# A weight load cut in two, later numerators and paired first tiles in a linear-attention and MoE kernel

## The chip, the cores and the metric

The kernel runs on one core of a Trainium2 chip. The metric is the device time of one execution in microseconds (us), taken as the median of several executions.

TensorE is called PE below, VectorE DVE, ScalarE ACT, and GpSimd POOL. L387 is line 387 of the kernel. The changed kernel has a few lines more, so later lines move (L444 is L447 there, L608 is L618), but the lines that matter here, L164 to L396, are the same in both.

## The reference

```python
phi(x) = where(x > 0, x, exp(x) - 1) + 1
q_p, k_p = phi(q), phi(k)                       # q, k, v: 8 batches, 8 heads, 576, 64
kv  = einsum('bhsd,bhse->bhde', k_p, v);  z = sum(k_p, axis=2)
num = einsum('bhsd,bhde->bhse', q_p, kv)
den = einsum('bhsd,bhd->bhs', q_p, z)[..., None] + 1e-6
x   = (num / den), as 4608 tokens x 512
h   = x @ w_in                                  # 512 x 2048
out = (h - tanh(h)) @ w_out                     # 2048 x 512
```

## The kernel before

The 4608 tokens go through the two dense layers in 9 chunks of 512. A chunk has 16 slots of layer 1 (a tile of 128 hidden features each, four matmuls over the pieces p of xT) and 16 slots of layer 2 (four matmuls each). The attention of later batches is hung onto these slots as lists of functions, `s1` and `s2`, so that PE always has dense matmuls between the small attention steps.

All inputs are loaded by POOL's queue, in the order in which they are issued (order of the first 25 us, cut):

```python
load_k(1); load_wo(0); load_wo(1); load_q(1)
...
load_v(1)
load_wo(2)          # w_out rows 1024..1535: the third quarter, features fi = 8..11
load_wo(3)
```

Layer 2 of chunk 0 goes quarter by quarter over four output tiles; later chunks go tile by tile. Before the third quarter stands the attention of batch 1:

```python
s2[7].append(lambda: (a_qT_pe(1, 0, side), a_kv(1, side), a_qT_pe(1, 1, side)))
...
for s in range(16):
    (g, i) = divmod(s, 4) if c == 0 else (s % 4, s // 4)
    ...
    l2mm(gT, os_[i], i, 4 * g, 4 * g + 4)     # four matmuls, L387
    if g == 3:
        evac(c, i, os_[i])                    # ACT copy, L396, then the store
    for f in s2[s]:
        f()
```

`a_qT_pe` transposes q (L164) and `a_kv` multiplies k and v (L177). In chunk 1 the numerators of batch 2 are made in slots 11 to 15, each a matmul into one of two PSUM banks (L317; four small ones, L320, for the last) and a DVE multiply by the reciprocal denominators `rdb`, which gives xT (L328):

```python
for p in range(NP + 1):
    s2[(11 if c == 1 else 9) + p].append(lambda p=p: a_num(n1, p))
```

`rdb` comes by way of DRAM: den, reciprocal on DVE (L285), four small stores `ds<-rden`, two spreading loads `rdb<-ds`. ACT also makes the exp of batch 2 in the last slots of chunk 0:

```python
s2[11].append(lambda: (exp2(qs, q_t, qp_t, "qp", 0), rest2(qs[0])))
s2[12].append(lambda: exp2(qs, q_t, qp_t, "qp", 1))
s2[13].append(lambda: (spread1(1), exp2(ks, k_t, kp_t, "kp", 0), rest2(qs[1]), a_qT_dma(2)))
s2[14].append(lambda: rest2(ks[0]))
```

## Time and profile before

| | before |
|---|---|
| median, at first | 294.08 us (3 runs, 293.90 to 294.33) |
| span of the profiled execution | 291.8 us |
| PE busy | 97% |
| late starts of PE that the change aims at | 0.22 us and 0.26 us |

The prediction below shows the lines. A late start is read like this: take the times at which two consecutive matmuls of PE start, subtract the usual spacing for that width (0.216 us for 512 columns, 0.056 us for 128), and what is left is lost. The `[idle before]` of the timeline is smaller than that or missing, because it counts from the modelled end of a matmul, 0.16 us after the next one could have started.

### The profile page before, as it was taken

What the parts mean: (1) busy time and instruction counts of PE and PEld (TensorE: products, weight loads), DVE (VectorE), ACT (ScalarE), POOL (GpSimd) and SP (SyncE); (2) the same over time, 40 slices, a digit from 0 to 9 for tenths busy, and PEclk for the clock granted to TensorE, in tenths of its full rate; (3) what the DMA queues carried; (4) which work ended last, traced back from release to release, by engine and by line L of the source; (5) the groups of instructions that cost most, each with busy time, mean ns of one, the idle gap of its engine ahead of it and who ended that gap; (6) DMA issues with size and microseconds to landing.
All of it is one profiled execution on the core that took longest, in us unless ns stands there. A gap on an engine that the chain in (4) does not pass through costs nothing.

```text
span 291.8 us, 4476 instructions
## 1 busy us (share of the span) xinstructions
PE 284.2 (97%) x1775; PEld 134.5 (46%) x1803; DVE 174.8 (60%) x266; ACT 139.7 (48%) x168; POOL 33.1 (11%) x55
## 2 busy tenths in 40 slices
PE   8999999999999999999999999999999999999994
PEld 3544464454454444544444445444444444444443
DVE  4759958987458674776478637865581457106600
ACT  4838638846254733465345534751551155126411
POOL 8673030110030003000300030000000000000000
PEclk9999999999999999999999999999999999999999
DMA  6999999998989668955795579766117310130032
GB/s 96 198 204 212 208 207 213 214 168 145 253 158 159 170 131 135 200 139 127 134 223 131 120 137 196 144 142 139 32 34 168 73 36 0 42 84 20 0 74 72
DMA packets 39077, 38.94 MB, mean 133 GB/s; under 512 B 16336, under 2 KB 33808, under 8 KB 38288
## 3 DMA queue, kind: packets, MB, share of 16 engines
q0 software_dynamic: 17552, 18.35, 39.0%
q1 hardware_dynamic: 21344, 20.17, 30.5%
q8 instruction: 14, 0.23, 0.3%
q10 hardware_dynamic: 160, 0.13, 0.1%
q14 instruction: 7, 0.06, 0.1%
HBM read 43.91 MB, written 9.55 MB: 183 GB/s over the span
## 4 chain that ended last, share of the span: by engine, by line
PE 75%; DMA 18%; POOL 2%; issue 1%; SPq 1%; DVE 1%; ACT 1%; DVEq 0%; POOLq 0%
PE ps_all L366 37%; PE ps_all L387 32%; DMA w_out_sb<-in_moe_w_out_dram 6%; DMA w_in_sb<-in_moe_w_in_dram 3%; DMA rdb<-ds 3%; DMA out_dram<-osb 2%; PE ps_all L199 2%; DMA kraw<-in_k_dram 2%; PE ps_all L317 2%; DMA ds<-rden 1%; PE ps_all L276 1%; POOL v L419 1%; ACT osb L396 1%; SPq L401 0%; POOL qraw L90 0%
## 5 line engine op out<-in xcount | busy, mean ns | idle before, releaser
L366 PE MATMUL ps_all<-xT,w_in_sb 128*128 128x512 bf16 x558 | 126.5, 380 | 0.9 <-issue 0.2
L387 PE MATMUL ps_all<-w_out_sb,gT 128*128 128x512 bf16 x548 | 126.2, 380 | 0.7
L373 DVE TENSOR_TENSOR gT<-ps_all,th 128x1024 bf16<-128x1024 f32 x64 | 77.9, 1218 | 59.7 <-ACT th L372 59.7
L372 ACT ACTIVATE th<-ps_all 128x1024 f32<-128x1024 f32 x64 | 65.5, 1023 | 57.0 <-PE ps_all L366 46.4
L366 PEld LDWEIGHTS <-w_in_sb 128*128 128x128 bf16 x574 | 55.0, 98 | 66.0
L387 PEld LDWEIGHTS <-gT 128*128 128x128 bf16 x560 | 54.1, 98 | 64.7 <-issue 0.6
L396 ACT COPY osb<-ps_all 128x512 f32<-128x512 f32 (+1 forms) x36 | 20.8, 582 | 72.3 <-PE ps_all L387 55.9
L328 DVE TENSOR_TENSOR xT<-ps_all,rdb 128x512 bf16<-128x512 f32 x24 | 16.3, 689 | 13.7 <-PE ps_all L317 11.2
L134 ACT ACTIVATE e<-qraw 128x1152 bf16<-128x1152 bf16 x16 | 18.5, 1161 | 7.3 <-DMA qraw<-in_q_dram 7.3
L134 ACT ACTIVATE e<-kraw 128x1152 bf16<-128x1152 bf16 x15 | 17.4, 1162 | 0.1
L136 DVE TENSOR_TENSOR qp<-e,r 128x1152 bf16<-128x1152 bf16 x16 | 12.1, 758 | 7.8 <-ACT e L134 7.0
L136 DVE TENSOR_TENSOR kp<-e,r 128x1152 bf16<-128x1152 bf16 x15 | 11.4, 758 | 7.9 <-ACT e L134 7.0
L383 POOL COPY g<-qT 1x1 bf16<-1x1 bf16 x5 | 0.9, 182 | 119.7 <-DMA qT<-qp 119.7
L378 DVE TENSOR_TENSOR gT<-ps_all,th 128x512 bf16<-128x512 f32 x16 | 10.3, 686 | 2.3 <-ACT th L377 1.7
L377 ACT ACTIVATE th<-ps_all 128x512 f32<-128x512 f32 x16 | 9.2, 598 | 4.4 <-PE ps_all L366 3.2
L444 PE MATMUL ps_all<-zero 128*128 128x512 bf16 x29 | 9.3, 487 | 1.2 <-DVE zero L405 1.2
L317 PE MATMUL ps_all<-qT,kz 128*128 128x512 bf16 x28 | 10.1, 380 | 0.1
L135 DVE TENSOR_SCALAR r<-qraw 128x1152 bf16<-128x1152 bf16 x16 | 7.3, 453 | 1.9 <-DMA qraw<-in_q_dram 1.9
L199 PEld LDWEIGHTS <-kp 64*128 64x128 bf16 x216 | 6.4, 94 | 2.5 <-issue 2.5
L285 DVE RECIPROCAL rden<-den 128x144 f32<-128x144 f32 x7 | 7.4, 1052 | 0.2
L199 PE MATMUL ps_all<-vp,kp 64*128 64x136 bf16 x216 | 7.4, 220 | 0.0
L394 DVE COPY osb<-ps_all 128x128 f32<-128x128 f32 x1 | 0.3, 291 | 11.6 <-DMA out_dram<-osb 11.6
(84 smaller groups left out, 123.0 us busy)
## 6 DMA issues: line engine op xcount, KB each, us to landing
out_dram<-osb SPq DMA_DIRECT2D x70, 128.0 KB
rdb<-ds SPq DMA_DIRECT2D x12, 576.0 KB
kraw<-in_k_dram POOLq DMA_DIRECT2D x7, 576.0 KB, 7.1
qraw<-in_q_dram POOLq DMA_DIRECT2D x7, 576.0 KB, 9.2
v<-in_v_dram POOLq DMA_DIRECT2D x7, 576.0 KB, 11.9
w_out_sb<-in_moe_w_out_dram POOLq DMA_DIRECT2D x4, 512.0 KB, 16.0
w_in_sb<-in_moe_w_in_dram POOLq DMA_DIRECT2D x6, 256.0 KB, 8.6
qraw<-in_q_dram POOLq DMA_DIRECT2D x2, 288.0 KB, 4.4
```

What stands on the lines that cost most here:

```text
L134: return (lambda: nc.scalar.activation(e, x, AF.Exp), lambda: nc.vector.tensor_scalar(r, x, 0.0, 1.0, ALU.max, ALU.add), lambda: nc.vector ...
L136: lambda: nc.vector.tensor_tensor(y, e, r, ALU.min))
L199: nc.tensor.matmul(ps[hg][:, i, :], kp[r, i, j].rearrange("p h d -> p (h d)"), vp[r, i, j, :], start=(j == 0), stop=(j == J - 1))
L317: nc.tensor.matmul(ps, kz[:, p // 2, p % 2, 0:128], qT[:, p % 2, 0:8, p // 2, :], start=True, stop=True)
L328: nc.vector.tensor_mul(xT[:, p, S * b:S * b + 512].rearrange("p (j t c) -> p j t c", j=8, t=4), ps.rearrange("p j (t c) -> p j t c", t=4), ...
L366: nc.tensor.matmul(h, w_in_sb[:, 2 * (p % 2) + p // 2, fi * 128:(fi + 1) * 128], xT[:, p, c * 512:(c + 1) * 512], start=(n == 0), stop=(n ...
L372: nc.scalar.activation(th, h, AF.Tanh)
L373: nc.vector.tensor_sub(gT[:, fi:fi + 2, :], h, th)
L378: nc.vector.tensor_sub(gT[:, fi, :], h, th)
L387: nc.tensor.matmul(o, gT[:, fi, i * 128:(i + 1) * 128], w_out_sb[:, fi, :], start=(fi == 0), stop=(fi == NF - 1))
L396: nc.scalar.copy(osb[:, f0:f1], o[:, f0:f1])
L444: nc.tensor.matmul(ps_all[:, 0, :], zero[:, 0:128], zero, start=True, stop=True)
```

## The change

Its intent is to take two short waits away from PE: one on the third quarter of w_out, one on the PSUM bank of a numerator. The pairs in chunk 2 are to keep the second step from making a new wait.

```diff
-    load_wo(2)
+    for n in range(2):
+        nc.gpsimd.dma_start(out=w_out_sb[:, 8 + 2 * n:10 + 2 * n, :],
+                            in_=moe_w_out[1024 + 256 * n:1280 + 256 * n, :].rearrange("(ko ki) f -> ki ko f", ki=128))
     load_wo(3)
@@
-                s2[(11 if c == 1 else 9) + p].append(lambda p=p: a_num(n1, p))
+                s2[min(12 + p, 15) if c == 1 else 9 + p].append(lambda p=p: a_num(n1, p))
@@
-            for p in range(NP):
-                l1mm(c, fi, h, p, p)
+            if c == 2 and fi == 1:
+                for two in (0, 2):
+                    for f, o in ((0, ps_all[:, dense.order[(dense.n - 2) % 6], :]), (1, h)):
+                        for p in (two, two + 1):
+                            l1mm(c, f, o, p, p)
+            elif c != 2 or fi > 1:
+                for p in range(NP):
+                    l1mm(c, fi, h, p, p)
@@
-            l2mm(gT, os_[i], i, 4 * g, 4 * g + 4)
+            if c == 0 and g == 2:
+                for n in (2 * i, 2 * i + 1):
+                    f = 8 + 2 * (n // 4)
+                    l2mm(gT, os_[n % 4], n % 4, f, f + 2)
+            else:
+                l2mm(gT, os_[i], i, 4 * g, 4 * g + 4)
```

## The prediction

> **What bounds the kernel now.** I read the page first: busy shares, then the chain that ended last. The page says PE is busy 97% of 291.8 us, and a busy PE here is a streaming PE, so I looked next at how far apart its matmuls start. Any gain must come out of places where PE does not start a matmul when it could.
>
> From the page of the kernel before, part 1 and part 4:
>
> ```profile
> PE 284.2 (97%) x1775; PEld 134.5 (46%) x1803; DVE 174.8 (60%) x266; ACT 139.7 (48%) x168; POOL 33.1 (11%) x55
> ...
> PE 75%; DMA 18%; POOL 2%; issue 1%; SPq 1%; DVE 1%; ACT 1%; DVEq 0%; POOLq 0%
> ```
>
> The DMA 18% in the chain looks like a lot, but a step of the chain can be 17.8 us long and have ended a wait of a fifth of a microsecond. So the waits of PE themselves come next (waiter, releaser, total us, times, longest):
>
> ```profile
> PE ps_all L444 <- DVE zero L405: 1.2, 1, 1.2
> PE ps_all L221 <- DMA v<-in_v_dram: 0.4, 1, 0.4
> PE ps_all L240 <- DVE xT L244: 0.2, 1, 0.2
> PE ps_all L366 <- issue: 0.2, 1, 0.2
> ```
>
> All of PE's listed waits are 2.0 us, and none of the four is one that the change touches. Its two waits are smaller, because the modelled end of a pipelined matmul (380 ns) hides most of them. Consecutive 512-column matmuls start 0.216 us apart (76.33 to 77.20: four of them, 0.87 us); 128-column transposes start 0.056 us apart. Against that spacing the PE timeline shows two late starts; the chain of waits names what released them.
>
> PE timeline, layer 2 of chunk 0 (start, duration, instruction):
>
> ```profile
> 40.20 0.68 PE L164 MATMUL ps_all<-ident,qp 128*128 128x128 bf16 x9
> 40.93 1.02 PE L387 MATMUL ps_all<-w_out_sb,gT 128*128 128x512 bf16 x3
> ```
>
> Chain of waits around it:
>
> ```profile
> 23.05 17.84 DMA w_out_sb<-in_moe_w_out_dram
> 40.89 0.04 issue
> 40.93 0.38 PE ps_all L387
> ```
>
> The ninth transpose starts at 40.65, so the layer 2 matmul could start at 40.71. It starts at 40.93, 0.04 us after the third quarter of w_out lands at 40.89: **0.22 us lost**.
>
> PE timeline and chain, end of layer 2 of chunk 1:
>
> ```profile
> 77.41 1.03 PE L387 MATMUL ps_all<-w_out_sb,gT 128*128 128x512 bf16 x4
> 78.54 0.38 PE L317 MATMUL ps_all<-qT,kz 128*128 128x512 bf16 x1
> ...
> 69.80 7.88 DMA rdb<-ds
> ...
> 77.80 0.70 DVE xT L328
> 78.50 0.04 issue
> 78.54 0.38 PE ps_all L317
> ```
>
> The fourth of those matmuls starts at 78.06, so the numerator matmul (third of batch 2) could start at 78.28. It starts at 78.54: **0.26 us lost**. It wants one of two PSUM banks, that bank is freed by the first L328, and L328 waited for rdb, which landed at 77.68. In chunk 2 the numerators start at 105.01, 106.09, 107.17 and 108.25, five matmuls apart, with no gap. Intervals of 0.432 us elsewhere are one missing matmul record each, not waits: there are 1775 matmuls against 1803 weight loads.
>
> **What the Trainium skill says.** "TensorE: Matmul & The Clock Gate", section "Wait — 56ns, not 53.3ns?", gives 215.7 and 55.6 ns start to start for warm matmuls of 512 and 128 columns; the trace agrees (216 and 56 ns), so those spacings are the floor that I measure gaps against. "DMA: Bandwidth & Descriptors", section "Anatomy of one DMA — SWDGE (gpsimd) path", puts a fixed cost of some 2.0 us on a DMA, mostly completion latency. In this trace it does not add up in a queue: w_in pieces, queued one behind the other, land at 23.02 and 24.32, 1.30 us apart for 256 KB on the chip. "Perfetto Trace Analysis", section "DMA Optimizations", says that splitting may let some work start sooner if the engines are generally idle; here they are busy (90% or more in most slices up to 40 us), so the half comes sooner only by its place in the queue.
>
> **The change, part by part.** The number of PE, ACT and SP instructions does not change. POOL gets one more DMA issue.
>
> Part 1, w_out's third quarter in halves. Landings in the trace: v of batch 1 at 38.38, third quarter 40.89, fourth 43.42, so a quarter takes 2.5 us and a half 1.26 to 1.30. The first half should land at 38.38 + 1.3 = 39.7, a microsecond before 40.71. Its eight matmuls in slot 8 and 9 (both halves of the tiles 0 to 3) need only it; the second half, at about 40.9 to 41.0, is first needed after them in slot 10, which began at 44.23. The fourth quarter at 43.5 is needed at 46.8. The extra issue costs 0.75 us of POOL at 24.5, which is idle from there to 38. **Gain 0.22 us**. Not all of it may reach the next chunk. Batch 2's q lands at 46.87 whatever PE does, and ACT is busy without a break from 46.95 on (exp, eviction, exp, and so on): its eviction that frees the bank of chunk 1's third tile ends at 51.66, so PE may enter at 51.71, where it now enters at 51.92. With 0.22 off that is 51.70: just touching. The split DMA may push q some 0.04 us later. I count 0.03 to 0.06 lost: **net 0.17**.
>
> Part 2, numerators of batch 2 a slot later (slots 12 to 15 for slots 11 to 15; the last two share slot 15). On the shifted clock the five would run at 76.8, 77.9, 78.9, 80.0 and 80.2. The third needs its bank at 78.54: 0.4 us of slack where there was a wait. The fourth needs the second evacuation (79.1), the fifth the third (about 80.1, 0.1 us of slack). **Gain 0.26 us**.
>
> Part 3, the first two tiles of chunk 2 by pairs. It pays for part 2. The last xT evacuation now starts at about 80.45 (fourth numerator 80.02 + 0.38 + 0.04, with a vp copy of 0.45 ahead of it on DVE) and ends at 81.15. Chunk 2 begins at about 80.35; in the old order xT piece 3 would be read 0.65 us later, at 81.0, a wait of 0.2 us. By pairs it is the sixth matmul that reads it, at 80.35 + 5 x 0.216 = 81.43 (the fifth reads piece 2, at 81.2, done by 80.1). Slack 0.2 us. The same 8 matmuls, and tanh of the pair comes after both either way: **cost 0**.
>
> Sum: 0.17 + 0.26 = **0.43 us** earlier at the start of chunk 2. From there PE streams without a wait to the end of the last layer 2, and everything else follows PE, so the end moves by the same. 294.08 - 0.43 = **293.65 us**, 0.15%.
>
> **The rivals.**
> A. A wait that takes the place of the first one: ACT, held by q's landing at 46.87, keeps the bank of chunk 1's third tile (or DVE that of tile 8: freed 56.77, now entered at 57.10, at 56.88 if all 0.22 carries). For it: margins of 0.0 and 0.05 us. Against: even if it takes all, part 2 stays. Then 293.8.
> B. The later numerators make xT late and PE waits at the head of chunk 2. For it: DVE has copies between the evacuations. Against: 0.2 us of slack by pairs. If rdb also lands later than 77.7 because traffic shifts, up to 0.3 us come back: 293.9.
> C. The split moves nothing, as DMA shares its engines between pieces and both halves land near 40.9. Against: landings come in issue order, 2.25 to 2.9 us apart, so the queue drains piece by piece. It would leave 293.85.
> D. A different number of DMAs shifts all later loads to another semaphore in the ring of eight that they use in turn, so that a load waits for another predecessor. For it: the order of loads. Against: the loads from batch 2 on are issued at 38.36 or later, when everything up to v of batch 1 has landed, or at 57 and later; and the fourth quarter's new predecessor, w_in's last piece, landed at 24.32, before its issue. No cost.
>
> **Range and chances.** The parts can give between 0 and 0.5 us. The three runs of before span 293.9 to 294.33, and the profiled run gave 293.62, so a median moves by 0.2 to 0.3 by itself, more than half of the effect. Range 293.1 to 294.3. A change of 2% would be 5.9 us; no wait concerned is over 0.3 us. Faster by over 2%: 0.01; within 2%: 0.98; slower: 0.01.
>
> **What would show it right or wrong.** In the changed profile: the layer 2 matmul after the second group of transposes starts 0.056 us after the last of them, and the chain has no w_out step there (part 1); w_out's first half lands near 39.7 (rival C if near 40.9); the spacing around the numerator matmuls in slots 12 to 15 of chunk 1 is 0.216 (part 2); no PE gap in the first 8 matmuls of chunk 2 (part 3, rival B); the start of chunk 1's third tile against the end of its bank's eviction (rival A). From chunk 2 on the timeline should be the old one moved by about 0.4 us. It would be wrong by more than noise if a load of a later batch came late by semaphore order, or if the two interleaved accumulations started more than 0.216 us apart; in chunk 0 interleaved tiles already start at that spacing.

## The result, and the profile after

The changed kernel took 293.57 us (median of 5 runs, 293.36 to 293.66) against 294.08 us (5 runs, 293.43 to 294.33). The ratio is 0.9985, 95% interval 0.9970 to 0.9999. The predicted time was 293.65 us, so the sum of the forecast came close; but the interval allows a gain of anything from 0.03 to 0.88 us. The two profiled executions, though, have the same span of 291.8 us, and the lines show why the sum is not the whole story.

The page of the changed kernel, parts 1 and 4:

```profile
PE 285.5 (98%) x1803; PEld 134.5 (46%) x1803; DVE 175.1 (60%) x266; ACT 139.7 (48%) x168; POOL 33.7 (12%) x56
...
PE 85%; DMA 11%; POOL 2%; issue 1%; DVE 0%; POOLq 0%
```

DMA in the chain fell from 18% to 11%. There are 28 more matmuls, but not because the program has more: the first profile lacked 28 records. PE's waits and its timeline in layer 2 of chunk 0, and the chain there:

```profile
PE ps_all L177 <- DMA v<-in_v_dram: 0.2, 1, 0.2
```

```profile
38.87 1.66 PE L177 MATMUL ps_all<-v,kp 64*128 64x192 bf16 x36 [0.22 <-DMA v<-in_v_dram]
40.46 0.68 PE L164 MATMUL ps_all<-ident,qp 128*128 128x128 bf16 x9
40.98 1.03 PE L387 MATMUL ps_all<-w_out_sb,gT 128*128 128x512 bf16 x4
```

```profile
22.32 16.50 DMA v<-in_v_dram
38.83 0.04 issue
38.87 1.66 PE ps_all L177 x36
```

Layer 2 now starts 0.52 us after the first of the nine transposes, without a wait: the wait on w_out is gone. But a new one stands 2 us ahead of it, on v of batch 1. v landed at 38.83 in this execution and at 38.38 in that of before, although it was issued at the same time (22.32) and ahead of the DMA that the change adds. The lost time there is 0.29 us (beyond the 0.10 us that this switch of tile shapes takes in every profile).

The numerators of chunk 1 and the head of chunk 2, PE timeline:

```profile
77.16 0.38 PE L317 MATMUL ps_all<-qT,kz 128*128 128x512 bf16 x1
...
78.23 0.38 PE L317 MATMUL ps_all<-qT,kz 128*128 128x512 bf16 x1
...
79.31 0.38 PE L317 MATMUL ps_all<-qT,kz 128*128 128x512 bf16 x1
...
80.39 0.38 PE L317 MATMUL ps_all<-qT,kz 128*128 128x512 bf16 x1
80.61 0.28 PE L320 MATMUL ps_all<-qT,kz 128*128 128x64 bf16 x4
```

They are 1.08 us apart, five matmuls, with no gap, and the first tiles of chunk 2 follow from 80.72 at the usual spacing. ACT's timeline around the end of chunk 0, in the profile of before (one line) and in that of after:

```profile
46.95 1.16 ACT L134 ACTIVATE e<-qraw 128x1152 bf16<-128x1152 bf16 x1 [1.06 <-DMA qraw<-in_q_dram]
```

```profile
47.34 1.16 ACT L134 ACTIVATE e<-qraw 128x1152 bf16<-128x1152 bf16 x1 [1.40 <-DMA qraw<-in_q_dram]
...
51.47 1.07 ACT L396 COPY osb<-ps_all 128x512 f32<-128x512 f32 x2
```

q of batch 2 landed at 47.25, 0.38 us later than in the profile of before, and ACT was busy without a break from then to the evictions. The first of this pair ended at 52.05, and the third tile of chunk 1 started at 52.10, 0.14 us late. This is the wait of the forecast's rival A, but not by its route: PE was ready for the tile at 51.96, no earlier than in the profile of before (51.92). The bank was late because q was.

So in this one pair of profiles the changed kernel lost 0.29 + 0.14 us to DMA landings and gained 0.23 + 0.27 us: 0.06 us between the first tanh of chunk 0 and the fourth of chunk 2, where the medians say 0.5 us in all. Either the change makes its own new waits, or a single profile is a sample of landings that vary. The experiments had to tell these apart.

### The profile page after: what moved, and what is told of

The parts are those of the page before. It is cut to its first block, busy times and chain, and to the rows that moved or that the text cites. A ratio compares the mean times of both kernels' runs of the same rounds, so it can differ in the third digit from the quotient of the medians.

```text
span 291.8 us, 4505 instructions
## 1 busy us (share of the span) xinstructions
PE 285.5 (98%) x1803; PEld 134.5 (46%) x1803; DVE 175.1 (60%) x266; ACT 139.7 (48%) x168; POOL 33.7 (12%) x56
## 4 chain that ended last, share of the span: by engine, by line
PE 85%; DMA 11%; POOL 2%; issue 1%; DVE 0%; POOLq 0%
PE ps_all L387 39%; PE ps_all L366 38%; DMA v<-in_v_dram 6%; DMA w_in_sb<-in_moe_w_in_dram 3%; PE ps_all L199 2%; DMA kraw<-in_k_dram 2%; PE ps_all L317 2%; PE ps_all L618 1%; PE ps_all L276 1%; POOL v L419 1%; PE ps_all L177 1%; POOL qraw L90 0%; PE ps_all L320 0%; POOL qraw L93 0%; POOL w_out_sb L115 0%
## 5 line engine op out<-in xcount | busy, mean ns | idle before, releaser
L387 PE MATMUL ps_all<-w_out_sb,gT 128*128 128x512 bf16 x560 | 127.5, 379 | 0.0
```

The source lines that it names most:

```text
L387: nc.tensor.matmul(o, gT[:, fi, i * 128:(i + 1) * 128], w_out_sb[:, fi, :], start=(fi == 0), stop=(fi == NF - 1))
```

## The experiments

The theory: how late each load lands depends on the slowest of the DMA engines that carry it and varies from one execution to the next by some 0.4 us; the change takes away the w_out wait whatever the landing, and the numerator wait where it occurs. The first rival: the added DMA itself delays the loads. The second: the gain is all in one part. Twelve runs were made in three calls (the first and third on one chip, the second on another), each with a profile and four to six timed executions against 9 or 11 of before. Eight of the nine executions of before in the third call are those of the first call, a quarter of an hour earlier, so its ratios lean on the chip staying the same; the changed kernel took 293.42 us in the first call and 293.36 us in the third. All gave correct results. In all, 14 profiles.

**Before, unchanged.**

> The kernel before, unchanged, for a second profile and as a measure of the noise: ratio 1.000 within 0.0015. In its profile the two late starts stand again: 0.26 us ahead of the third numerator matmul of batch 2, and some 0.2 us ahead of layer 2's ninth group in chunk 0. Theory one (the slowest of the 16 engines of each load differs from run to run, by some 0.4 us): v of batch 1 lands anywhere between 38.3 and 38.9 and the third quarter of w_out 2.5 us after it, so the second late start is 0.2 to 0.7 us in all, with v's share. Theory two (the added DMA of the changed kernel makes the loads late): v lands at 38.4 as in the first profile, within 0.1.

Measured: ratio 0.9994 (0.9981 to 1.0006). Timeline of PE in chunk 0 of this second profile of before, and the numerators of chunk 1:

```profile
40.42 0.68 PE L164 MATMUL ps_all<-ident,qp 128*128 128x128 bf16 x9
41.32 1.02 PE L387 MATMUL ps_all<-w_out_sb,gT 128*128 128x512 bf16 x4 [0.23 <-DMA w_out_sb<-in_moe_w_out_dram]
```

```profile
77.59 0.38 PE L317 MATMUL ps_all<-qT,kz 128*128 128x512 bf16 x1
...
78.67 0.38 PE L317 MATMUL ps_all<-qT,kz 128*128 128x512 bf16 x1
```

The w_out wait is there again, and larger: 41.32 less 40.42 is 0.90 us, where nine transposes need 0.50, so 0.39 us (to the trace's rounding) against 0.23. The wait ahead of the third numerator, expected to stand again, is **not** there: 78.67 is 1.08 us after 77.59. My expectation missed here. v landed at 38.76 with no added DMA in the program.

**After, unchanged, twice.**

> The changed kernel, unchanged, for a second profile. Ratio to before 0.9985 by the sum of its parts. Theory one: v of batch 1 lands anywhere between 38.3 and 38.9, so PE's wait for it is 0 to 0.3 us, not the 0.29 us of the first profile again. Theory two: v lands at 38.8 again and the wait is 0.3 us again. Either way no gap at the numerators of batch 2 and none at the head of chunk 2.

> The changed kernel a third time, as the measure of the other three of this call. Ratio to before 0.998 to 0.9985. Waits in its profile: 0 to 0.3 us on v of batch 1, 0 to 0.15 us at the third tile of chunk 1, none on w_out, none at the numerators, none in the first 8 matmuls of chunk 2.

Measured: ratios 0.9980 (0.9966 to 0.9993) and 0.9978 (0.9966 to 0.9991). The second profile has no late start of any of these kinds at all; v landed at 38.62, in time for PE, whose first tanh of chunk 0 came 0.46 us later than in the first profile. The third has 0.30 us on v (landed 38.71), 0.09 us on the transposes behind q of batch 1, and 0.27 us on the bank of chunk 1's third tile. None has a wait on w_out, at the numerators or at the head of chunk 2.

**Part 1 alone: the halves.**

```diff
-    load_wo(2)
+    (two halves, as in the change)
-            l2mm(gT, os_[i], i, 4 * g, 4 * g + 4)
+            (half by half in chunk 0, as in the change)
```

> Only the w_out quarter in halves and its use half by half. Theory one: the wait on w_out is gone, the 0.26 us gap at the numerators in chunk 1 stays; 0 to 0.2 us faster than before as v's landing falls, ratio about 0.9995. Theory two (v always late by 0.45 us with this DMA): no gain or 0.15 us slower, ratio 1.000 to 1.0005, v at 38.8.

Measured: ratio 0.9985 (0.9972 to 0.9997), more than either theory had it. PE timeline:

```profile
40.41 0.68 PE L164 MATMUL ps_all<-ident,qp 128*128 128x128 bf16 x9
40.92 0.81 PE L387 MATMUL ps_all<-w_out_sb,gT 128*128 128x512 bf16 x3
```

No wait on w_out, and none on v, which landed at 38.47 with the added DMA in the program. And although the numerators are in their old slots, the gap ahead of the third is 0.02 us, not 0.26. Halves at 39.79 and 41.04: the forecast's 39.7 and 40.9 to 41.0 hold.

**Parts 2 and 3 alone: later numerators and pairs.**

> Only the later numerators and the pairs in chunk 2. The 0.26 us gap is gone, the wait on w_out of about 0.2 us stays; from chunk 2 on 0.26 us ahead of a run of before with the same landings; ratio 0.9991. If the whole gain of the change were in part 1, as a rival has it, this one is at 1.000.

Measured: ratio 0.9989 (0.9977 to 1.0002). In its profile v landed late (39.09) and w_out at 41.61:

```profile
39.14 1.66 PE L177 MATMUL ps_all<-v,kp 64*128 64x192 bf16 x36 [0.23 <-DMA v<-in_v_dram]
40.73 0.68 PE L164 MATMUL ps_all<-ident,qp 128*128 128x128 bf16 x9
41.66 0.59 PE L387 MATMUL ps_all<-w_out_sb,gT 128*128 128x512 bf16 x2 [0.25 <-DMA w_out_sb<-in_moe_w_out_dram]
```

The v wait of 0.30 us stands here **without** any part of the split. That is the clearest single line against the rival of the added DMA. By time alone the parts cannot be ranked: the intervals overlap, and the two gains (0.0015 and 0.0011) add to more than each of the three measured gains of the whole (0.0015, 0.0020, 0.0022).

**The split without the new order of use.**

```diff
-    load_wo(2)
+    (two halves, as in the change; used tile by tile as before)
```

> The kernel before with the third quarter of w_out as two DMAs, but used whole, tile by tile, as before. If the gain of part 1 comes from the first half's earlier landing, the group's first two matmuls start without a wait at about 40.7 to 41.1, and the third, 0.43 us later, wants the second half, which lands at 41.0 to 41.3: a wait of 0 to 0.2 us is left, so most of part 1's gain without the new order of use; ratio 0.9987 to 0.9995. If an added DMA made all loads later (the rival), v would land 14.5 us after w_in's last piece rather than the 14.1 to 14.2 of the kernel before, and the ratio would be 1.000 or over.

Measured: ratio 0.9989 (0.9975 to 1.0003); the interval includes 1. v landed 14.14 us after w_in's last piece. No w_out wait is left (second half at 41.12, wanted at 41.19); 0.18 us on v and 0.16 us on the bank. The order of use looked idle here; a later run says otherwise.

**Later numerators without the pairs.**

> The kernel before with the later numerators alone, without the pairs in chunk 2. By my working xT piece 3 is then read by the fourth matmul of chunk 2, some 0.18 us before it is ready: one gap of 0.1 to 0.25 us there, none at the numerators. If the pairs are idle, no gap. Time: 0 to 0.1 us from before, ratio 0.9995 to 1.0005.

Measured: ratio 0.9999 (0.9986 to 1.0011). PE and DVE at the head of chunk 2:

```profile
81.28 2.07 PE L366 MATMUL ps_all<-xT,w_in_sb 128*128 128x512 bf16 x8
```

```profile
81.36 0.69 DVE L328 TENSOR_TENSOR xT<-ps_all,rdb 128x512 bf16<-128x512 f32 x1
```

Eight matmuls at the usual spacing take 7 x 0.216 + 0.38 = 1.89 us; these took 2.07. The 0.18 us sit ahead of the fourth, at 82.11, which reads the xT that DVE finished at 82.05. This is the 0.2 us that the forecast worked out for the old order, and no profile with the pairs has it.

**Numerators a slot earlier.** A dose in the other direction.

```diff
-                s2[(11 if c == 1 else 9) + p].append(lambda p=p: a_num(n1, p))
+                s2[(10 if c == 1 else 9) + p].append(lambda p=p: a_num(n1, p))
```

> The kernel before with the numerators of batch 2 a slot EARLIER (slots 10 to 14). In the profiles so far rdb lets the first evacuation start 13.6 to 13.9 us after the reciprocal ended, and the third numerator came 14.4 us after it. A slot earlier it comes 13.3 us after it, and must wait until 13.6 + 0.7 + 0.05 = 14.35 or later: a gap of 1.0 to 1.3 us there, ratio 1.0035 to 1.0045. If the gap of the first profile had another cause than rdb (a rival), this costs nothing.

Measured: ratio 1.0030 (1.0016 to 1.0043). PE timeline:

```profile
76.74 0.38 PE L317 MATMUL ps_all<-qT,kz 128*128 128x512 bf16 x1
76.95 1.03 PE L387 MATMUL ps_all<-w_out_sb,gT 128*128 128x512 bf16 x4
78.69 0.38 PE L317 MATMUL ps_all<-qT,kz 128*128 128x512 bf16 x1 [0.70 <-DVE xT L328]
```

The gap is 0.87 us (0.70 us after the modelled end), a little under the 1.0 to 1.3 expected, as the third numerator would have come 13.5 us after the reciprocal, not 13.3. The mechanism stands: the third numerator waits for the first evacuation, and that for rdb.

**v of batch 1 in halves as well, on top of the change.**

```diff
-        load(b, v_b[b % 2][:, 0:2], v, b == 0)
+        load(b, v_b[b % 2][:, 0:2], v, b <= 1)
```

> The changed kernel with batch 1's v loaded in two halves as well. The first half should land 1.4 us before the second, near 37.3, so that the matmuls that read v at 38.6 never wait for it, however late its slowest engine is; the second half (38.4 to 39.1) is wanted at 39.4. Against the changed kernel: 0 to 0.3 us faster, 0.1 on the mean, ratio to before 0.9978. If the time of the changed kernel is set by something else, equal to it.

Measured: ratio 0.9980 (0.9966 to 0.9993), not to be told from the changed kernel. The halves landed at 37.50 and 38.91. PE had no late start, as also in one of the three profiles of the changed kernel.

**The exp of batch 2's first k half after the eviction, on top of the change.**

```diff
-            s2[13].append(lambda: (spread1(1), exp2(ks, k_t, kp_t, "kp", 0), rest2(qs[1]), a_qT_dma(2)))
-            s2[14].append(lambda: rest2(ks[0]))
+            s2[13].append(lambda: (spread1(1), rest2(qs[1]), a_qT_dma(2)))
+            s2[14].append(lambda: (exp2(ks, k_t, kp_t, "kp", 0), rest2(ks[0])))
```

> The changed kernel with the exp of batch 2's first k half a slot later, so that ACT evicts chunk 0's third tile before it, not after. That bank should be free some 1.1 us earlier (about 50.7 to 51.0) and the third tile of chunk 1 never waits for it: against the changed kernel 0 to 0.15 us faster, by how late q of batch 2 lands. If that gap has another cause, it stays where it is in profiles with a late q.

Measured: ratio 0.9983 (0.9970 to 0.9995). ACT's pair of evictions in the third profile of the changed kernel, and PE's first tiles there:

```profile
51.49 1.07 ACT L396 COPY osb<-ps_all 128x512 f32<-128x512 f32 x2
```

```profile
50.78 2.58 PE L366 MATMUL ps_all<-xT,w_in_sb 128*128 128x512 bf16 x10
```

Ten matmuls need 9 x 0.216 + 0.38 = 2.32 us; 0.26 us more is the wait for the bank, whose eviction ended at 52.07. With the exp later it is the second and the third tile of chunk 0 that are evicted one after the other, and the third one's eviction ends at 50.58:

```profile
49.51 1.06 ACT L396 COPY osb<-ps_all 128x512 f32<-128x512 f32 x2
```

There is no wait at chunk 1's third tile in this profile or in the two below. But q of batch 2 landed at 46.80 to 46.84 in all three, early enough that the old order would not have waited either, so the missing wait proves nothing. What is shown is that the bank is free sooner: by 1.5 us, of which 0.44 us is the earlier q and some 1.05 us the later exp. The v wait of 0.24 us remained.

**Both of these together, and the same with the old order of use.**

> The changed kernel with v of batch 1 in halves and the later exp together: no PE wait between the chunk 0 transposes and chunk 2 but the 0.1 us for the spread of batch 1. Against the changed kernel 0 to 0.4 us, 0.15 on the mean; ratio to before about 0.9975.

> As the last one, but the third quarter of w_out, still loaded as two DMAs, is used whole, tile by tile, as before the change. If the order of use is idle, as the run with the split alone suggested, equal to the last one within 0.1 us; if it is needed, a wait of up to 0.4 us at the third matmul of the group, where the second half lands late.

Measured: 293.22 and 293.19 us, both ratios 0.9974 (0.9960 to 0.9987, and 0.9960 to 0.9988). These are the fastest versions and clear of noise against before. Against the changed kernel (293.36 us) they are 0.15 us ahead by the medians, which the runs cannot settle. For the first I had expected no wait from the transposes of chunk 0 on; its profile has one just ahead of them. Its chain:

```profile
19.98 15.99 DMA qraw<-in_q_dram
...
37.18 0.77 DVE qp L136
37.95 0.05 issue
38.00 0.68 PE ps_all L164 x9
```

The transposes now wait 0.24 us for q of batch 1, the load ahead of v. And with the old order of use:

```profile
40.49 1.24 PE L387 MATMUL ps_all<-w_out_sb,gT 128*128 128x512 bf16 x4
```

Four matmuls need 1.03 us; the 0.22 us more are a wait of the third for w_out's second half, which landed at 41.10. So the new order of use is not idle in every execution: in the profile of the split alone it had nothing to save, and here, with PE early, it would have saved 0.22 us. The timed runs of the two orders, 293.22 and 293.19 us, do not tell them apart.

## Why the prediction was right, and where it was not

All late starts by kind, from the trace, in us. The stretch goes from the end of chunk 0's first tanh to the end of chunk 2's fourth; the last column is the stretch less the waits.

| profile | w_out | numerators | v | q (transposes) | bank of third tile | head of chunk 2 | stretch | less waits |
|---|---|---|---|---|---|---|---|---|
| before | 0.23 | 0.27 | | | | | 69.33 | 68.84 |
| before, second | 0.39 | | | | | | 69.24 | 68.85 |
| parts 2 and 3 | 0.42 | | 0.30 | 0.03 | | | 69.60 | 68.85 |
| part 2 | 0.40 | | 0.09 | | | 0.18 | 69.51 | 68.84 |
| slot earlier | 0.31 | 0.87 | | | | | 70.02 | 68.84 |
| after | | | 0.29 | | 0.14 | | 69.27 | 68.84 |
| after, second | | | | | | | 68.84 | 68.84 |
| after, third | | | 0.30 | 0.09 | 0.27 | | 69.52 | 68.86 |
| part 1 | | 0.02 | | | | | 68.87 | 68.84 |
| split alone | | | 0.18 | | 0.16 | | 69.18 | 68.84 |
| v in halves | | | | | | | 68.85 | 68.85 |
| exp later | | | 0.24 | | | | 69.09 | 68.85 |
| both | | | | 0.24 | | | 69.09 | 68.86 |
| both, old order | 0.22 | | | | | | 69.06 | 68.84 |

The last column is the same within 0.02 us in 14 profiles of 11 programs. From there to the end takes 201.58 to 201.66 us in all of them. So from the first tanh on, the waits in the table are the whole of what differs between these executions. (The 20.64 to 21.36 us before it lie outside the account. They end before any edited instruction runs, and vary between executions by more than the gain.) The forecast's claim that PE streams unhindered from chunk 2 on is shown.

**Part 1, net 0.17: right in kind, both of its terms mis-sized.** The gross 0.22 was one sample; the five profiles with a whole quarter have 0.23 to 0.42, mean 0.35. The step that failed is reading one gap as the gap. The deduction for rival A (0.03 to 0.06) was too small as well: the bank cost 0.14, 0 and 0.27 us in the three profiles of the changed kernel. The forecast took q of batch 2 to land at 46.87 "whatever PE does", or some 0.04 us later by the split; it landed at 47.25, 47.25 and 47.27. The three costs differ only by when PE arrives (51.96, 52.13 and 51.86, against a bank free at 52.05 to 52.07).

**Does the split itself make q of batch 2 late?** That rival was not tested, and the record leans towards it. q landed at 46.65 to 46.96 in the five profiles without the split, at 47.03 to 47.27 in five of the six with the split and a whole v (46.83 in the other), and at 46.80 to 46.86 in the three with v in halves too. All three bank waits stand in the second group, and none would stand with q at 46.87. Only the last few of the transfer's 16 semaphore increments are late; the eighth comes at 45.3 to 45.7 in all 14. Nothing here shows why. If it is the split, then the split gives back a part of what it gains.

**A wait that the forecast did not list: v of batch 1.** It cannot be put down to the split: it is there in two profiles without it (0.30 and 0.09) and absent in two of the six with a split w_out and a whole v. v's landing after w_in's last piece was 13.96 to 14.23 us in the five profiles without the split, and 14.14 to 14.30 in four with it; 14.56 in the first profile after and 13.70 in the one with the later exp are the extremes. On the clock of the execution v landed at 38.83 on the mean of the five without the split and at 38.70 on that of the six. A shift of a tenth by the added DMA is not excluded, one of 0.45 us finds no support. What varies most is the slowest of the 16 parts of the transfer. The eighth of v's 16 semaphore increments came between 37.3 and 37.8 in every profile with v whole, the last between 38.38 and 39.12. Which engine it is, and why it trails, the traces do not tell.

**Part 2, 0.26: mis-sized.** The mechanism is right (the slot 10 run), but the old slot stood on the edge of it. The third numerator comes 14.39 us after the reciprocal; it waits if the first evacuation starts more than 14.39 - 0.74 = 13.65 us after it. In the four profiles with the old slot the gap was 0.27, 0.00, 0.02 and 0.00, as their evacuations' starts (13.91, 13.58, 13.66 and 13.50 us) ask; in the slot 10 run the same sum, 13.64 + 0.74 - 13.52, gives 0.86 where 0.87 was seen. From the evacuation's start in all 14 profiles (13.50 to 14.12 us) I estimate a mean gap of about 0.14 us; what that is in timed runs stays open. The first profile happened to show a bad case.

**Part 3, cost 0 and 0.2 us saved: right.** No profile with the pairs has a gap there, and without them it was 0.18 us.

**Rivals.** A occurred in two of the three profiles of the changed kernel, by a later q and not, as the forecast had it, by an earlier PE. B did not with the pairs, and did without them. C fell: the two halves land 1.24 to 1.28 us apart, the first before PE comes. D cost nothing that shows, but not for the reason given: the fourth quarter's issue did wait for w_in's last piece (landed 24.27, issued 24.55 in the first profile after; 25.24 and 25.53 in the one with the later exp). It landed 2.54 to 2.60 us behind its predecessor all the same, and the tail of 201.6 us is untouched. Whether the late q of batch 2 is a form of D stays open.

That the sum, 0.43, is close to the measured 0.51 by the medians is in part luck. From the waits in the profiles I estimate 0.35 for w_out and 0.14 for the numerators, less 0.14 for the bank (the mean of 0.14, 0 and 0.27): 0.35 us, within the measured interval of 0.03 to 0.88 as well. The profiles of before and after alone would show less: their mean stretches, 69.29 and 69.21 us, differ by 0.08. Two and three executions are too few for that mean, and those of before were fast ones (293.62 and 293.73 us, where its timed runs reach 294.60). That the waits fall away is shown; how the timed half microsecond divides among them is not.

## What to carry to other kernels

Gaps of a few tenths of a microsecond behind a DMA in a single profile can be samples of a landing that varies; profile the unchanged kernel twice before giving such a gap a size, and put two profiles through a full account (stretch less waits) before believing a cause. Not every late landing is chance, though: q of batch 2 came late in all three profiles of the changed kernel and in neither of before, so compare every load, not only the one that was cut. Here a queue of loads paced the stream, and splitting the load that PE waited for paid although the DMA engines were busy, as the needed bytes came earlier in the queue (39.79 to 40.21 for the first half, 40.89 to 41.62 for the whole quarter); but waits on other loads, v and q, stood close behind, so the gain was capped. When work is moved later to free a bank, check its next reader: here reordering eight matmuls kept 0.18 us from coming back.

## What the Trainium skill lacked or had wrong

- "DMA: Bandwidth & Descriptors", section "Why a DMA increments its semaphore by 16 and not by 1", says that only the full 16 means that the data landed. It gives no time by which the slowest part trails. Here the last of the 16 increments of the 576 KB load of v came 0.9 to 1.6 us after the eighth, and its time moved by 0.7 us between executions.
- The same page, section "Anatomy of one DMA — SWDGE (gpsimd) path", gives a fixed cost of about 2.0 us for each DMA. It does not say that DMAs queued one behind the other do not each pay it. Here it does not show between them: the whole quarter of w_out landed 2.50 to 2.52 us after its predecessor, each half 1.24 to 1.32 us after its predecessor.
- "Perfetto Trace Analysis", section "DMA Optimizations", says that splitting may let some DMAs start sooner, and ties a sooner end of the whole task to DMA engines that are generally idle. It does not speak of busy engines. Here they were 90% busy or more in most slices up to 40 us, and the split still removed waits of 0.23 to 0.42 us.
- "Perfetto Trace Analysis" does not say that single matmul records can be missing from a trace: 5 of the 14 profiles have 1775 matmuls for 1803 weight loads, and each missing one looks like a gap of 0.216 us.
